# One written order for a whole fused attention and two-layer MLP program, in place of a written head and a scheduled rest

## The chip, the cores and the metric

The kernel runs on one core of a Trainium2 chip. The metric is device microseconds of one execution. The kernel before has a median of 858.6 us over three runs.

## The reference, cut to what matters

Nyström attention feeds two dense layers. Sizes: 4 batches, 8 heads, 576 positions, head size 64; 2304 tokens, width 512, inner width 2048.

```python
q_lm = q.reshape(B, H, 32, 18, D).mean(axis=3)
k_lm = k.reshape(B, H, 32, 18, D).mean(axis=3)
A, Bm, C = sm(q, k_lm), sm(q_lm, k_lm), sm(q_lm, k)   # row softmax, scale 1/8
Z = Bm.T / (norm1(Bm) * norminf(Bm) + 1e-6)
for _ in range(6):
    Z = 2 * Z - Z @ Bm @ Z
x = A @ Z @ C @ v            # heads side by side: [2304, 512]
h = x @ w_in;  g = h * tanh(softplus(h));  x = g @ w_out
h = x @ w2_in; g = relu(h) ** 2;           out = g @ w2_out
```

## The kernel before, in words

**Products.** The two MLP layers work on pairs of reduced-precision fp32 parts, a high and a low one ("h" and "l" in the tile names). Each product is three matmuls into one PSUM accumulation: high by high, low by high, high by low (`prod`, L685 to L687; the second layer's second product writes them out in L771 to L773).

**Attention.** Each batch has two groups of four heads; the eight groups are called a to h. A group's steps are: load q, k, v (`lq`, `lk`, `lv`), landmark sums on VectorE (`sq`, `sk`, L312 and L318), transposes on TensorE (`tq`, `tk`, `tl`) with ScalarE copies (`Tq`, `Tk`, `TL`), the three score products (`pa`, `pb`, `pc`), and the softmax pieces on VectorE, ScalarE and GpSimd (`at`, `am`, `mi`, `ae`, `su`, `mu`, `tb` for A; `cm`, `ce`, `cr`, `pe`, `ET`, `pv`, `cv` for C with v). `ah` and `al` split A into the two parts. A batch (B0 to B3) does the six Newton steps (`bx`, `be`, `bs`, `nr`, `rs`, then `n0` to `n5` on TensorE with `r` on ScalarE and `z` on VectorE) and `pw`, `wz`, which make the 64 x 64 factor of each head.

**Folds.** The product with w_in of the first layer is not made from x: each batch's small factors are multiplied into w_in, for each of four column groups of 512 (`Fold`, F00 to F33: batch, column group). `fo` is eight calls of a 64 x 32 by 64 x 512 matmul (L662, 16 instructions in the trace), on different parts of the array; `mh` (ScalarE, L670) and `ml` (VectorE, L673) split the result.

**Turns.** The MLP work is 48 turns, t0 to t23 for layer one, t24 to t47 for layer two. A turn is one column group (512 of 2048) and one block of 384 tokens. Its four `f` steps make h in PSUM (two banks, each for two f); `M` is the activation on ScalarE (L737), `c` and `g` split it (L746 or L749 on ScalarE, L755 on VectorE, with a square on VectorE, L747, in layer two). The `y` steps (four in layer one, three in layer two) multiply with w_out into a PSUM buffer of which there are two, shared with attention steps; `e` adds it to an accumulator in SBUF (L793, L795, L797). The last column group of layer one also splits x (L804 on ScalarE, L805 on GpSimd), that of layer two also stores (four DMAs, L811).

**Weights.** 64 weight units (U0 to U63: for each layer and column group four of w_in and four of w_out) come in a raw 64-bit form. `d` loads 512 KB on SP's queue; `lo` (ScalarE, L200), `st` (VectorE, L203), `ab` (ScalarE L210, or VectorE L212 when the unit is "beside"), `cl` (VectorE, L216 and L217) and `ad` (GpSimd, L223 or L227) turn them into fp32; `hi` (ScalarE, L232) and `lw` (GpSimd, L238) split them. The raw form has two buffers of its own; the split parts have 24.

**Who orders the work.** Every engine takes its instructions in order, and SP's queue issues the loads and stores in order. In the kernel before, the list `PROGRAM` (641 steps) gives the order by hand up to the last f of turn 7; each word is a thing, a step, behind "@" the PSUM buffer and behind "+" a number of extra matmuls that keep TensorE going. Then a loop over turns 8 to 47 emits folds (`folded`), fronts (f, M, c, g), backs (y, e) and, by the due times in `WHEN`, weight units from 16 on (`wturn`, whole units through `all`). What stands outside `tc.manual_schedule()` is put in order by the framework's scheduler, by a timeline that it works out itself; it may place these instructions between those of the list.

Of the kernel before, what the change touches and what calls it, by code (L numbers as in the profile page):

```python
# [46 lines left out]


PROGRAM = """
    a.lk U0.d@m a.lq a.sk a.tk@h a.Tk U1.d@m a.Sk U0.lo a.lv a.sq a.tq@h a.Tq b.lk U0.st a.Sq U1.lo a.tl@y U0.ab  # L50
    U2.d@m U1.st a.TL U0.cl U1.ab a.pb@y b.lq a.pa@at b.sk U0.ad a.PB a.pc@h U3.d@m U2.lo b.tk@h a.cm b.Sk a.at
    a.ce b.lv a.am b.Tk a.pe@at a.cr a.mi b.sq U4.d b.tq@h a.ET a.ae a.pv@y c.lk b.Tq a.su a.cv b.Sq U2.st U3.lo
    b.tl@y U5.d a.mu U2.ab b.TL c.lq a.tb U4.lo b.pc@h+4 U3.st a.ah b.pb@at U4.st U6.d@gh c.tk@h+3 U3.ab U2.cl
    U4.ab a.al b.cm b.PB U5.lo c.lv c.tq@at+2 c.sk b.ce U2.ad c.Tq b.pe@h d.lk U6.lo b.pa@at B0.bx U4.cl B0.be
    U7.d@gl b.ET B0.bs c.Sk b.pv@y+1 c.Tk b.at U4.ad d.lq B0.nr@y b.am U4.hi d.tk@h B0.rs U7.lo d.Tk U1.cl
    B0.n0@at+5 d.lv d.tq@h U4.lw B0.r0 B0.z0 c.sq B0.n1@y d.Tq b.mi U8.d B0.r1 U1.ad B0.z1 b.ae b.cr B0.n2@at+2
    d.sq e.lk b.cv B0.r2 c.Sq c.tl@y c.TL B0.z2 b.su B0.n3@y+2 U8.lo c.pb@at e.lq B0.r3 e.tk@h B0.z3 c.PB U7.st
    d.Sq U3.cl B0.n4@y U7.ab c.pc@h b.mu B0.r4 B0.z4 d.sk B0.n5@y c.pa@at U3.ad f.lk e.Tk B0.z5 e.lv d.Sk U7.cl
    B0.pw@y+3 d.tl@y B0.wz U7.ad b.tb F00.fo@h f.lq d.TL c.at U7.hi d.pb@y c.am b.ah d.pc@at U7.lw c.cm F00.mh
    d.cm b.al c.ce f.lv F00.ml d.ce f.tk@h+4 c.mi c.cr d.PB d.cr t0.f0 f.Tk B1.bx U5.st d.pe@at c.ae U6.st B1.be  # L60
    t0.f1 d.ET c.su U6.ab d.pv@y B1.bs x.m t0.M0 t0.f2 U6.cl B1.nr@y e.sq d.cv U6.ad t0.c0 d.pa@at c.mu c.pe@h
    U6.hi x.e U5.ab t0.f3 B1.rs d.at U6.lw B1.n0@y+2 e.Sq c.ET B1.z0 f.tq@at d.am B1.r0 x.m t0.M1 U5.cl B1.n1@y
    c.pv@y d.mi B1.z1 c.tb t0.c1 e.tq@h t0.g0 B1.r1 c.cv t0.g1 B1.n2@y x.e d.ae B1.z2 U5.ad e.sk B1.r2 U5.hi
    B1.n3@y+4 U5.lw B1.r3 B1.z3 d.su e.Sk f.Tq B1.n4@y+3 e.tl@y U9.d B1.r4 B1.z4 c.ah d.mu f.sk B1.n5@at t0.y0
    e.Tq c.al e.TL d.tb t0.y1 t0.e0 B1.z5 U9.lo U8.st f.Sk d.ah U9.st B1.pw@y U8.ab f.sq d.al e.pc@h t0.e1
    e.pb@at U9.ab t0.y2 e.PB B1.wz f.Sq U9.cl F10.fo@h e.cm t0.e2 U9.ad f.tl@at F10.mh U8.cl U10.d t0.y3 f.TL
    U8.ad F10.ml e.ce f.pa@at t0.e3 e.cr f.pc@h f.at U11.d U10.lo e.pe@h f.cm e.pa@at e.ET U10.st f.pb@y g.lk
    f.ce f.am e.pv@y f.PB f.mi U10.ab f.cr f.pe@h e.at U11.lo t1.f0 U10.cl f.ae f.ET B2.bx t1.f1 g.lq f.su
    U10.ad B2.be e.cv g.tk@at x.m t1.M0 B2.bs U12.d t1.f2 f.mu g.sk t1.c0 g.lv B2.nr@y f.pv@y g.Tk f.tb t1.f3
    f.cv t1.g0 g.Sk U12.lo t2.f0 t1.M1 U12.st t1.c1 g.tq@at U11.st x.e U11.ab t2.f1 t1.g1 e.am t1.y0 B2.rs x.m  # L70
    t2.M0 U11.cl B2.n0@y t2.f2 B2.z0 t2.c0 g.sq U11.ad t2.f3 t1.e0 e.mi U13.d B2.r0 g.Tq F01.fo@h t2.g0 x.e e.ae
    F11.fo@at t1.y1 F01.mh e.su F11.mh t1.y2 F01.ml e.mu t1.e1 x.m t2.M1 F11.ml B2.n1@y t3.f0 B2.z1 e.tb B2.r1
    t2.c1 B2.n2@at t3.f1 B2.z2 B2.r2 t2.g1 e.ah t3.f2 f.ah e.al B2.n3@y t1.e2 t3.f3 B2.z3 B2.r3 U13.lo f.al
    B2.n4@at t3.M1 t1.y3 B2.z4 B2.r4 x.e U12.ab U13.st t2.y0 U13.ab U12.cl t1.e3 U13.cl g.Sq t2.y1 t2.e0 U13.ad
    x.m t3.M0 U12.ad t4.f0 U13.hi B2.n5@at t2.e1 U13.lw t4.f1 U12.hi t3.c0 B2.z5 t4.f2 U14.d t3.c1 U12.lw t4.f3
    t3.g0 B2.pw@y t3.g1 t4.M0 t2.y2 B2.wz U15.d U14.lo t4.M1 U14.st F20.fo@at x.e U14.ab g.tl@y t5.f0 U15.lo
    U14.cl t5.f1 F20.mh U15.st t5.f2 U14.ad F20.ml U15.ab t5.f3 g.TL U15.cl U14.hi g.pa@at t2.e2 U15.ad t2.y3
    g.at h.lk U14.lw U15.hi g.am g.pb@y U15.lw t2.e3 g.pc@at t4.c0 g.cm g.mi h.lq t4.c1 t3.y0 h.sk g.ce g.ae
    h.tk@at g.PB t3.e0 h.Sk t3.y1 h.Tk h.lv h.sq h.tq@at t3.e1 h.Sq g.su h.tl@y h.Tq t3.y2 h.TL t4.g0 t4.g1 x.m
# [850 lines left out]
```

## Time and profile before

| What | Value |
|---|---|
| median of three runs | 858.6 us (857.69 to 862.78) |
| profiled execution, span | 856.0 us |
| granted TensorE clock, mean | 0.995 |
| TensorE busy | 818.3 us |
| VectorE busy | 455.4 us |
| ScalarE busy | 363.9 us |
| GpSimd busy | 198.1 us |

The span goes from the first to the last instruction of one execution. PE is TensorE's matmuls, PEld its weight loads, DVE VectorE, ACT ScalarE, POOL GpSimd, SP SyncE, which issues the DMAs. Matmuls are pipelined, so the duration of one is longer than the distance to the next; starts are compared, not durations.

### The profile page before, as it was taken

The page shows a single profiled execution, that of the slowest core. Times are in us where ns is not written, and L with a number is a line of the kernel's source. Part 1 is how long each engine was busy: PE and PEld are TensorE (multiplying, and loading weights), DVE is VectorE, ACT ScalarE, POOL GpSimd, SP SyncE. Part 2 cuts the span into 40 slices and gives each one's busy share as a digit, 9 for nine tenths or more (in the row PEclk, how much of TensorE's full clock was granted, in tenths as well). Part 3 has the DMA queues.
Part 4 walks back from the last instruction along what each step waited for, and adds up shares of the span by engine and source line. Part 5 has one row for each costly group of instructions (what it writes and reads, how often), then busy time and mean ns, then how long its engine had stood idle before and what let it go on. Part 6 is the DMA issues. An engine that isn't in the chain of part 4 may idle for free.

```text
span 856.0 us, 13523 instructions
## 1 busy us (share of the span) xinstructions
PE 818.3 (96%) x5646; PEld 732.6 (86%) x5646; DVE 455.4 (53%) x721; ACT 363.9 (43%) x578; POOL 198.1 (23%) x179
## 2 busy tenths in 40 slices
PE   4778999798999999999999999999999999999997
PEld 3657788687997989898999899899989989999996
DVE  5899865765346655247434633744345553534332
ACT  4668797643453434244734413533233421321120
POOL 1434323222032232016533301331023300300000
PEclk9999999999999999999999999999999999999999
DMA  9951503203033111011101100211011300101112
GB/s 245 312 164 27 158 27 129 53 3 99 1 99 99 50 50 50 1 50 50 50 1 50 50 1 28 72 49 50 1 50 50 99 0 1 50 1 50 50 50 74
DMA packets 25916, 53.29 MB, mean 62 GB/s; under 512 B 3072, under 2 KB 15360, under 8 KB 25856
## 3 DMA queue, kind: packets, MB, share of 16 engines
...
q14 instruction: 16, 0.13, 0.0%
...
## 4 chain that ended last, share of the span: by engine, by line
PE 75%; DMA 9%; DVE 6%; issue 4%; POOL 2%; ACT 2%; SPq 1%; ACTq 0%; POOLq 0%; DVEq 0%
PE h L685 11%; PE h L687 11%; PE h L686 11%; PE y L772 8%; PE y L773 8%; PE y L771 8%; PE y L685 6%; PE y L686 6%; PE y L687 6%; DMA rawwo<-in_moe_w_out_dram 4%; DMA rawwi<-in_moe_w_in_dram 3%; DMA q<-in_q_dram 2%; PE m L662 2%; DVE gl L755 1%; SPq L192 1%
## 5 line engine op out<-in xcount | busy, mean ns | idle before, releaser
L737 ACT ACTIVATE s<-h 128x768 f32<-128x768 f32 x96 | 77.5, 807 | 189.4 <-PE h L687 186.0
L755 DVE TENSOR_TENSOR gl<-s,gh 128x768 fp32r<-128x768 f32 x96 | 97.6, 1020 | 40.9 <-ACT gh L749 40.3
L747 DVE TENSOR_TENSOR s<-s 128x768 f32<-128x768 f32 x48 | 47.5, 991 | 86.4 <-ACT gh L746 86.0
L685 PE MATMUL h<-ah,mh 128*128 128x384 f32 (+1 forms) x256 | 80.0, 313 | 0.0
L687 PE MATMUL h<-ah,ml 128*128 128x384 f32 (+1 forms) x256 | 78.4, 306 | 0.4 <-DVE ml L673 0.4
L686 PE MATMUL h<-al,mh 128*128 128x384 f32 (+1 forms) x256 | 78.0, 305 | 0.0
L797 DVE TENSOR_TENSOR o<-o,y 128x512 f32<-128x512 f32 x54 | 37.0, 685 | 70.0 <-PE y L773 69.2
L797 DVE TENSOR_TENSOR acc<-acc,y 128x384 f32<-128x384 f32 x72 | 39.3, 549 | 54.4 <-PE y L687 54.1
L227 POOL TENSOR_TENSOR rawwo<-rawwo 128x512 int32<-128x512 int32 x32 | 36.8, 1151 | 101.0 <-DVE rawwo L217 76.7
L685 PEld LDWEIGHTS h<-ah,mh 128*128 128x128 f32 x256 | 48.5, 190 | 6.0 <-issue 2.5
L687 PEld LDWEIGHTS h<-ah,ml 128*128 128x128 f32 x256 | 48.6, 190 | 2.4 <-issue 1.7
L686 PEld LDWEIGHTS h<-al,mh 128*128 128x128 f32 x256 | 48.6, 190 | 0.8 <-issue 0.8
L749 ACT CAST gh<-s 128x768 fp32r<-128x768 f32 x48 | 39.6, 834 | 18.7 <-PE y L687 17.9
L203 DVE SCALAR_TENSOR_TENSOR rawwo<-rawwo 128x512 uint32<-128x512 uint32 x32 | 26.7, 838 | 34.4 <-ACT rawwo L200 31.7
L203 DVE SCALAR_TENSOR_TENSOR rawwi<-rawwi 128x512 uint32<-128x512 uint32 x32 | 22.0, 687 | 39.2 <-ACT rawwi L200 36.6
L746 ACT ACTIVATE gh<-s 128x768 fp32r<-128x768 f32 x48 | 40.5, 845 | 1.2
L200 ACT ACTIVATE rawwi<-rawwi 128x512 f32<-128x512 uint32 x32 | 21.6, 675 | 43.1 <-DMA rawwi<-in_moe_w_in_dram 41.9
L200 ACT ACTIVATE rawwo<-rawwo 128x512 f32<-128x512 uint32 x32 | 21.7, 677 | 41.8 <-DMA rawwo<-in_moe_w_out_dram 41.7
L805 POOL TENSOR_TENSOR xl<-acc,xh 128x384 fp32r<-128x384 f32 x24 | 26.3, 1100 | 33.6 <-ACT xh L804 33.6
L223 POOL TENSOR_TENSOR wi<-rawwi 128x512 int32<-128x512 int32 x16 | 16.7, 1046 | 70.6 <-DVE rawwi L217 59.4
L227 POOL TENSOR_TENSOR rawwi<-rawwi 128x512 int32<-128x512 int32 x16 | 19.9, 1247 | 52.8 <-DVE rawwi L217 48.3
L662 PE MATMUL m<-wi,wz 64*32 64x512 f32 x256 | 24.5, 601 | 0.1
...
## 6 DMA issues: line engine op xcount, KB each, us to landing
rawwo<-in_moe_w_out_dram SPq DMA_DIRECT2D x32, 512.0 KB, 3.9
...
rawwi<-in_moe_w_in_dram SPq DMA_DIRECT2D x16, 512.0 KB, 3.7
...
k<-in_k_dram SPq DMA_DIRECT2D x4, 576.0 KB, 4.3
q<-in_q_dram SPq DMA_DIRECT2D x4, 576.0 KB, 6.5
...
```

The costliest lines, as they stand in the source:

```text
L203: nc.vector.scalar_tensor_tensor(self.low, self.up, 0x80000000, self.low, ALU.bitwise_and, ALU.bitwise_or)
L227: nc.gpsimd.tensor_tensor(up, up, low, ALU.add)
L685: nc.tensor.matmul(ps, wh, rh, start=start, stop=False)
L686: nc.tensor.matmul(ps, wh, rl, start=False, stop=False)
L687: nc.tensor.matmul(ps, wl, rh, start=False, stop=stop)
L737: nc.scalar.activation(s, self.hs[hf][:, :, :TT], AF.Relu if self.li else AF.Mish)
L747: nc.vector.tensor_tensor(s, s, s, ALU.mult)
L755: nc.vector.tensor_tensor(self.gl[:, sl, :], self.s[hf], self.gh[:, sl, :].bitcast(F32), ALU.subtract)
L771: nc.tensor.matmul(ps, gh, W.oh[f][:, 0, :], start=(i == 0), stop=False)
L772: nc.tensor.matmul(ps, gh, W.ol[f][:, 0, :], start=False, stop=False)
L773: nc.tensor.matmul(ps, gl, W.oh[f][:, 0, :], start=False, stop=(i == FG - 1))
L797: nc.vector.tensor_tensor(a, a, ps, ALU.add)
```

## The change

The loop, `WHEN`, `TURN`, `folded`, `wturn`, `front` and `back` go. `PROGRAM` now names all 1834 steps of the program, and all of it stands inside `tc.manual_schedule()`. Steps that had done work on two engines are cut: `q` (the square on VectorE) comes out of `c`; `xh` and `xl` (the split of x) and `o` (the stores) come out of `e`. `x.two` swaps the SBUF pools between the layers. Units 16 to 39 are marked "beside" (`ab` on VectorE); before, the loop marked those that it emitted in layer one. The head of the list is in a new order too: among other things the loads begin a.lq, a.lk, b.lk, U0, b.lq, U1, U4, U2, U3, c.lk, where they began a.lk, U0, a.lq, U1, a.lv, b.lk, U2, b.lq, U3, b.lv. No instruction of the computation is added or removed.

```diff
-TURN = 8
-WHEN = [
...
 PROGRAM = """
-    a.lk U0.d@m a.lq a.sk a.tk@h a.Tk U1.d@m a.Sk U0.lo a.lv a.sq a.tq@h a.Tq b.lk U0.st a.Sq U1.lo a.tl@y U0.ab
...
-    t7.M1 t7.c1 t7.g1 t6.y3 t6.e2 t6.e3
+    a.lq a.lk a.sq b.lk a.tq@h a.Sq a.Tq a.sk a.Sk U0.d@m b.lq U1.d@m a.tk@h a.tl@y a.Tk a.TL U0.lo a.pa@at U4.d
...
+    U15.lo h.lv B2.r4 U15.st t4.f1 U15.ab B2.n5@at t3.c1 U12.lw x.m B2.z5 t2.e1
...
+    t2.y3 t2.e2 U14.cl U17.d g.pc@at g.am g.cm U14.ad U14.hi t2.e3 t4.c0 t5.f3 U14.lw t3.y0 x.e h.Sk g.ce g.mi
+    U17.lo h.tk@at t3.e0 g.ae t4.g0 f.ah h.Tk t5.M1 t3.y1 h.tq@at f.al h.tl@y t3.e1 g.su g.mu h.Tq t3.y2 h.TL t3.e2
...
+    t18.y3 U34.st U34.ab U34.cl U34.ad U34.hi U34.lw t20.f3 t18.xl2 F33.fo@at t19.g1 F33.mh t19.y0 t20.c0 t18.e3
...
+    t47.c0 t43.o1 t47.q0 t46.y0 t46.y1 t47.c1 t46.e0 t47.g0 t46.e1 t47.q1 t46.y2 t47.g1 t46.e2 t46.o0 t47.y0 t47.y1
+    t47.e0 t46.o2 t47.e1 t47.y2 t46.o1 t47.o0 t47.o1 t47.e2 t47.o2
 """
...
-    def folded(b, fg):
-        if (b, fg) not in folds:
-            x = Fold(b, fg)
-            x.fo()
-            x.mh()
-            x.ml()
...
             if self.li:
                 nc.scalar.activation(gh, s, AF.Square)
-                nc.vector.tensor_tensor(s, s, s, ALU.mult)
...
+        def q(self, hf):
+            s = self.s[hf]
+            nc.vector.tensor_tensor(s, s, s, ALU.mult)
...
+        def xh(self, k):
...
+        def xl(self, k):
...
+        def o(self, k):
...
+        def two(self):
+            nonlocal l2
+            l1.release()
+            l2 = ctx.enter_context(tc.tile_pool(name="l2", bufs=NT, reuse_waits="tile"))
...
+    for u in units[16:BESIDE]:
+        u.beside = True
...
-    def wturn(t):
-        n = 16
-        for a, e in WHEN:
-            n += 4 if t >= e else max(0, min(4, math.ceil(4 * (t - a) / (e - a))))
-        while done[0] < min(n, len(units)) and len(free["w"]) > (not units[done[0]].by_rows):
-            units[done[0]].beside = t < len(ORDER)
-            units[done[0]].all()
-            done[0] += 1
...
-    for i, w in enumerate(turns + [None]):
...
```

## Rows read from the trace of the kernel before

**Rows 1.** The page's part 1: busy time, share of the span, instructions.

```profile
PE 818.3 (96%) x5646; PEld 732.6 (86%) x5646; DVE 455.4 (53%) x721; ACT 363.9 (43%) x578; POOL 198.1 (23%) x179
```

**Rows 2.** By stage: length, busy us of PE, PEld, DVE, ACT, POOL; clock; DMA.

```profile
0.00:60.19 60.19, 39.20 (x534) 28.44 (x535) 47.72 (x89) 33.95 (x72) 19.78 (x28) 1.00 0.91 256
60.19:106.20 46.01, 41.71 (x637) 34.65 (x636) 41.91 (x84) 36.21 (x72) 16.76 (x16) 0.96 0.32 85
106.20:206.00 99.80, 92.44 (x916) 78.84 (x916) 64.57 (x126) 63.95 (x114) 27.17 (x26) 0.98 0.20 57
206.00:280.00 74.00, 73.52 (x466) 67.18 (x467) 35.78 (x59) 34.65 (x51) 16.44 (x14) 1.00 0.26 72
280.00:851.40 571.40, 571.40 (x3100) 523.52 (x3098) 264.69 (x366) 195.12 (x270) 117.96 (x95) 1.00 0.13 40
```

**Rows 3.** TensorE's timeline around a whole fold: start us, us, line, out<-in.

```profile
406.76 0.34 PE L687 MATMUL h<-ah,ml 128*128 128x384 f32 x1
407.02 1.09 PE L662 MATMUL m<-wi,wz 64*32 64x512 f32 x16
...
408.32 0.34 PE L685 MATMUL h<-ah,mh 128*128 128x384 f32 x1
```

**Rows 4.** TensorE's timeline: first cut fold, one cut fold, the last one.

```profile
257.82 1.05 PE L662 MATMUL m<-wi,wz 64*32 64x512 f32 x4
...
300.23 0.34 PE L687 MATMUL h<-ah,ml 128*128 128x384 f32 x1
300.50 1.05 PE L662 MATMUL m<-wi,wz 64*32 64x512 f32 x4
...
301.76 0.34 PE L686 MATMUL y<-gl,wo_8h 128*128 128x384 f32 x1
...
305.60 0.34 PE L687 MATMUL y<-gh,wo_11l 128*128 128x384 f32 x1
305.87 1.08 PE L662 MATMUL m<-wi,wz 64*32 64x512 f32 x12
...
307.15 0.34 PE L686 MATMUL h<-al,mh 128*128 128x384 f32 x1
...
392.97 1.07 PE L662 MATMUL m<-wi,wz 64*32 64x512 f32 x10
```

**Rows 5.** VectorE's first sums, the loads' sizes (page, part 6), the weight step L203.

```profile
5.14 2.12 DVE L318 TENSOR_REDUCE lmk<-k 128x64 f32<-128x1152 f32 x1 [3.33 <-DMA k<-in_k_dram]
9.87 2.13 DVE L318 TENSOR_REDUCE lmq<-q 128x64 f32<-128x1152 f32 x1 [2.61 <-DMA q<-in_q_dram]
...
rawwi<-in_moe_w_in_dram SPq DMA_DIRECT2D x16, 512.0 KB, 3.7
...
q<-in_q_dram SPq DMA_DIRECT2D x4, 576.0 KB, 6.5
...
L203 DVE SCALAR_TENSOR_TENSOR rawwo<-rawwo 128x512 uint32<-128x512 uint32 x32 | 26.7, 838 | 34.4 <-ACT rawwo L200 31.7
```

**Rows 6.** Timelines of ScalarE and TensorE, 155 to 206 us; in brackets the wait before.

```profile
155.24 0.67 ACT L200 ACTIVATE rawwi<-rawwi 128x512 f32<-128x512 uint32 x1 [2.38 <-DMA rawwi<-in_moe_w_in_dram]
156.67 1.44 PE L346 MATMUL tk<-ident,k 128*128 128x128 f32 x8 [2.64 <-ACT E L424]
158.23 0.52 PE L686 MATMUL y<-gl,wo_4h 128*128 128x384 f32 x1
160.47 0.45 PE L687 MATMUL y<-gh,wo_6l 128*128 128x384 f32 x1
167.78 0.45 PE L685 MATMUL y<-gh,wo_4h 128*128 128x384 f32 x1 [2.05 <-DVE acc L797]
199.92 0.69 ACT L200 ACTIVATE rawwi<-rawwi 128x512 f32<-128x512 uint32 x1 [4.78 <-DMA rawwi<-in_moe_w_in_dram]
206.00 0.45 PE L685 MATMUL y<-gh,wo_0h 128*128 128x384 f32 x1 [2.26 <-DVE acc L797]
```

**Rows 7.** VectorE's last instruction.

```profile
851.44 0.69 DVE L797 TENSOR_TENSOR o<-o,y 128x512 f32<-128x512 f32 x1 [2.03 <-PE y L773]
```

More of the change, by code (lines that the diff above doesn't have):

```diff
@@ L32 @@
 NW = 24
+BESIDE = 40
 IN_PAGES = ((1, 0), (1, 1), (2, 0), (2, 1))
@@ L781, in e @@
             li, fg, n = self.li, self.fg, self.n
-            last = fg == NFG - 1
             ps = self.ys[k]
@@ L798, in e @@
             give(f"y{self.nm}{k}")
-            if last and li == 0:
-                if k % 2 == 0:
-                    for t, x in zip("hl", xs.setdefault(n, ([], []))):
-                        x.append(page(f"x{t}{n}{k // 2}", F32R))
-                xh, xl = (t[k // 2][:, k % 2, :] for t in xs[n])
-                nc.scalar.copy(xh, a)
-                nc.gpsimd.tensor_tensor(xl, a, xh.bitcast(F32), ALU.subtract)
-                if k % 2:
-                    give(f"acc{n}{k // 2}")
-            elif last:
-                for m in range(P // LM):
-                    b, i = divmod((n * TT + k * P) // LM + m, SEG)
-                    nc.sync.dma_start(
-                        out[b * S : (b + 1) * S, :].rearrange("(l i) d -> i l d", i=SEG)[i],
-                        a[m * LM : (m + 1) * LM, :],
-                    )
-        def front(self):
-            for k in range(FG):
-                self.f(k)
-                yield
-                if k % 2:
-                    self.M(k // 2)
-                    self.c(k // 2)
-                    self.g(k // 2)
-        def back(self):
-            for k in range(TT // P if self.li else NCC):
-                self.y(k)
-                self.e(k)
-                yield
+        def xh(self, k):
+            n = self.n
+            if k % 2 == 0:
+                for t, x in zip("hl", xs.setdefault(n, ([], []))):
+                    x.append(page(f"x{t}{n}{k // 2}", F32R))
+            nc.scalar.copy(xs[n][0][k // 2][:, k % 2, :], acc[n, k // 2][:, k % 2, :])
+        def xl(self, k):
+            n = self.n
+            xh, xl = (t[k // 2][:, k % 2, :] for t in xs[n])
+            nc.gpsimd.tensor_tensor(xl, acc[n, k // 2][:, k % 2, :], xh.bitcast(F32), ALU.subtract)
+            if k % 2:
+                give(f"acc{n}{k // 2}")
+        def o(self, k):
+            n, a = self.n, outs[self.n][:, k, :]
+            for m in range(P // LM):
+                b, i = divmod((n * TT + k * P) // LM + m, SEG)
+                nc.sync.dma_start(
+                    out[b * S : (b + 1) * S, :].rearrange("(l i) d -> i l d", i=SEG)[i],
+                    a[m * LM : (m + 1) * LM, :],
+                )
     class Tables:
@@ L852, in nystrom_mish_relu2 @@
     things["x"] = Tables()
+    for u in units[16:BESIDE]:
+        u.beside = True
+    l2 = None
     with tc.manual_schedule():
```

170 lines of the change are left out of this document (106 added, 64 removed).

## The prediction, made before the result was known

> **What bounds the kernel now.** I read the page's shares first. TensorE is busy 96% of the span, VectorE 53%, ScalarE 43% [rows 1]. In a kernel like this the only time that can be won without removing work is TensorE's idle time and the matmul time that is badly used, so the second view was busy time by stage [rows 2]. From 280.00 us to 851.40 us TensorE is busy for all 571.40 us of it: no order of the list can remove idle time there. The idle time lies in front. Up to 60.19 us, where the first layer-1 product starts, it is 60.19 - 39.20 = 21.0 us; then 46.01 - 41.71 = 4.3 us; then 99.80 - 92.44 = 7.4 us up to 206 us; then 0.5 us. The rest of the 856.0 us span is the tail: the last product ends near 851.4 us, VectorE adds it in 0.69 us, and its four stores land at the end, 4.6 us in all [rows 7]. The tail keeps its form in the new list (last y, last e, last o), so it cancels.
>
> VectorE is the engine behind the first two stages: it is busy 47.72 of 60.19 us and 41.91 of 46.01 us [rows 2]. What it is handed first decides when TensorE gets its products. In the third stage it has room (64.57 of 99.80 us), and what matters there is who stands in front of whom in its queue.
>
> **Term 1, the folds.** The third view was TensorE's own timeline. A fold's matmuls go to different 64x32 parts of the array side by side, so a fold costs the time of one part. Where a fold stands whole (x16), from the h in front of it at 406.76 to the second h behind it at 408.32 there are 1.56 us [rows 3]. Take off two product intervals. One interval is 0.1745 us: from 301.76 to 305.60 there are 22 products [rows 4]. A whole fold therefore costs 1.56 - 0.35 = 1.21 us. In the part that the scheduler orders, a fold is cut in two by a pair of y groups: a piece of x4 and a piece of x12. The x4 piece costs 301.76 - 300.23 - 0.35 = 1.18 us, the x12 piece 307.15 - 305.60 - 0.35 = 1.20 us [rows 4]. A piece costs as much as the whole. There are seven such cut folds of the sixteen, the first with its x4 at 257.82, the last with its x10 at 392.97 [rows 4]. In the new list `fo` is one step, its eight calls stand together in the written order, and TensorE takes them so. Gain: 7 x (1.18 + 1.20 - 1.21) = 7 x 1.17 = 8.2 us. All seven lie behind 206 us, where TensorE is idle for 0.5 us in all [rows 2], so nothing hides this; it is on the path. Bounds: 7 x 1.0 and 7 x 1.2.
>
> **Term 2, the start.** The old list issues a.lk, then 512 KB of weights (U0), then a.lq. VectorE gets k at 5.14 us and q only at 9.87 us, after an idle wait of 2.61 us [rows 5]. These two transfers of 512 and 576 KB take 4.73 us, 230 KB/us. The new list issues a.lq, a.lk, b.lk and then U0. The second tensor then comes 576/230 = 2.5 us after the first: 2.2 us earlier. Against that, more VectorE work is listed ahead of t0.f0: U5.st and U6.st have moved in front of it, 2 x 0.838 us [rows 5], and B1.bx, while c.cr and d.cr have moved behind. Two y weights alone take back 1.7 of the 2.2 us for the first product. Ahead of t1.f0 both lists have the same weight steps, and the new one has e.at, e.cr and f.cr behind it, so there the 2.2 us stand. I take 2.0 us. Bounds: a loss of 1.7 us (the loads gain nothing, the two steps cost) and a gain of 4.3 us (all the idle time of the second stage [rows 2]). The v loads move behind e.lk; pv is needed only for B0.pw, at the end of the Newton chain, which hides them.
>
> **Term 3, the stalls between 106 and 206 us.** Three gaps make up 6.9 of the 7.4 us. At 156.67 tk waited 2.64 us for E of ScalarE, at 167.78 a y waited 2.05 us and at 206.00 another 2.26 us for VectorE's acc [rows 6]. In front of the first and the last, ScalarE sat 2.38 and 4.78 us in front of `lo` (L200) of a w_in unit until its load landed [rows 6]. The last w_in unit of the old list is U11, and U12 to U15 are w_out: so these are units from 16 on, from the loop behind the list, which the scheduler moved up into it. ScalarE and VectorE take their work in order, so E and acc stood behind them. After the first gap the clock fell: from 158.23 to 160.47 seven products take 0.32 us each, where they take 0.1745 else [rows 6, 4]. That is about the half level, 1.2 against 2.4 GHz, with a granted clock of 0.98 over the whole stage [rows 2]. Ten such products lost 1.4 us. Together 6.9 + 1.4 = 8.3 us.
>
> The new list names every one of these units. U17.lo stands behind g.ce, and between the step that frees its buffer (U15.lw) and U17.lo there are 8.7 us of listed TensorE work; the tk of group h is no longer behind an unlanded load. h.lk stands 12 us of TensorE work ahead of h.tk. So I expect the three old gaps gone. But a list that names all units has its own tight places. Of the 48 units from 16 on, I count 16 with under 5 us of listed TensorE work between the step that frees the raw buffer and the `lo` (U34, U36, U42, U51, U59 and U61 have none), while L200 waits for landings of some 4 us. Each holds ScalarE, and VectorE behind it, until the load is there. Whether TensorE notices depends on the next acc: a y group lasts 2.72 us (0.69 us of e and 2.03 us of wait for the next [rows 7]), and two buffers stand between a y and the e that frees it. The bound from below is nothing, as after 280 us in the old trace, where such waits exist and TensorE never stops. The bound from above is 16 x 2.2 = 35 us at the price of one old gap. I take two new gaps of 2.2 us, because in the old trace such units made three gaps, all in the stage in which VectorE also has attention to do, and the new list has two of them (U16, U17) ahead of t6.f3, where that stage ends. Net: 8.3 - 4.4 = 3.9 us.
>
> **Edits at nothing.** Splitting q from c, xh and xl from e, and o from e moves no work to another engine and adds no instruction; L747 ran behind L746 before and has 3 us or more of products as cover. The warm matmuls are 35 in both lists. The set of ScalarE table loads changes by a few of 1.3 us, on an engine that is 57% idle. The order of the o steps at the end (t46.o2 ahead of t46.o1) makes SP wait for one e; three y groups of 2.72 us still stand between that e and the last one, as cover. BESIDE = 40 gives `ab` of units 16 to 39 to VectorE, as the loop did for units taken during the first layer's turns.
>
> **Sum.** 856.0 - 8.2 - 2.0 - 3.9 = 841.9 us of span. The median of the runs, 858.6 us, is 2.6 us above the profiled span; I carry that over: 844.5 us, 1.6% faster. About 1% is what a measurement of this kernel can tell from no change.
>
> **The clock as an added price.** After the 2.64 us gap the rows show about half rate for some 3 us, after the 2.26 us gap at 206 us they show none: the stage that begins there has a granted clock of 1.00 [rows 2, 6]. The Trainium skill (TensorE: Matmul & The Clock Gate, section "HAM oscillation — how this bites in real kernels") says that idle time between bursts sends the clock back to its half level, so that the next burst starts slow; the trace agrees at 157 us and not at 206 us. By that rule each of my two new gaps would also cost 1.4 us, and the sum would be 847.3 us.
>
> **Rivals.**
> *Only the folds.* The new gaps equal the old ones and the start gains nothing: 856.0 - 8.2 + 2.6 = 850.4 us. For it: old and new list are nearly alike up to t7.f0 in what stands ahead of what. Against it: the three gaps have a cause that the new order takes away.
> *All of it.* No new gap, and the whole idle time of the second stage goes: 856.0 - 8.2 - 4.3 - 8.3 + 2.6 = 837.8 us. For it: 571 us without a gap in the old trace although weights wait for loads there too.
> *Slower: weights hold the queues.* The 16 tight units each stop TensorE for 2.2 us, since a written order lets no later step pass a waiting `lo` or `st`. 856.0 - 8.2 - 2.0 - 8.3 + 35.2 + 2.6 = 875.3 us. It turns slower than before once 9 of the 16 do so (18.5 / 2.2 = 8.4). For it: L200's waits of 2.38 and 4.78 us in front of real gaps. Against it: y buffers and the room of VectorE after 206 us (it is busy 264.69 of 571.40 us [rows 2]).
> *The folds stay cut.* If the written order did not bind TensorE, term 1 would vanish: 852.7 us. Against it: the folds named in the old list are all x16.
>
> **Chances.** Forecast 0.50, only the folds 0.21, all of it 0.17, weights hold 0.10, folds stay cut 0.02. The forecast spreads over 839 to 850 us. Range 833 to 858 us: below, the "all of it" case and 5 us of the first stage's idle time; above, the folds alone with some new gaps. Faster by over 1% (under 850.0): nearly all of the forecast, "all of it" and a fifth of "only the folds", 0.70. Within 1%: 0.21. Slower by over 1%: 0.09.
>
> **What would show it.** Folds: sixteen pieces of x16, none of x4 to x12. Start: q and k on VectorE about 2.5 us apart, the first h at 58 to 60 us. Stalls: no TensorE wait of 2 us between 106 and 206 us with an L200 in front; idle time after 280 us not over 5 us. I am wrong if TensorE waits for acc or s in many places after 206 us, with L200 waiting for a load ahead of each, or if a fold's time in one piece is near 2.4 us.

## The result, and the profile after

The kernel after takes 825.13 us (median of four runs, 824.35 to 827.35); the kernel before took 858.14 us beside it (856.20 to 862.78). The ratio is 0.961, 95% interval 0.957 to 0.966. The prediction was 844.5 us with a range of 833 to 858: the sign was right, the gain of 33 us is more than twice the 14 us forecast, and it lies outside the range. The profiled span is 822.8 us, against 856.0.

The page's part 1 of the kernel after, to be read beside [rows 1]:

```profile
PE 802.0 (97%) x5646; PEld 730.1 (89%) x5646; DVE 447.1 (54%) x721; ACT 368.3 (45%) x588; POOL 201.7 (25%) x179
```

The same instructions on TensorE, and yet 16 us less busy time. The rest of the gain is idle time, and the view by stages tells where (columns as in [rows 2]; the stages are cut at the first layer-1 product and at like places behind it):

```profile
0.00:53.99 53.99, 38.38 (x535) 28.52 (x535) 47.11 (x86) 35.56 (x75) 18.33 (x27) 0.94 1.01 269
53.99:94.00 40.01, 39.41 (x576) 33.84 (x575) 35.10 (x79) 32.58 (x65) 17.52 (x16) 1.00 0.42 114
94.00:190.00 96.00, 96.00 (x1034) 84.87 (x1033) 65.48 (x131) 67.49 (x116) 30.38 (x28) 1.00 0.22 67
190.00:260.00 70.00, 70.00 (x464) 65.80 (x462) 33.85 (x52) 37.09 (x55) 12.59 (x10) 1.00 0.18 52
260.00:818.20 558.20, 558.18 (x3048) 517.03 (x3046) 264.82 (x375) 195.55 (x279) 122.88 (x98) 1.00 0.14 43
```

Length less TensorE's busy time, stage by stage, before and after: 21.0 and 15.6 us, 4.3 and 0.6, 7.4 and 0, 0.5 and 0. The first product begins at 53.99 us, 6.2 us earlier and ahead of the 58 to 60 us that the prediction gave as a sign. From 94 us to the end of its last product TensorE is idle for 0.02 us in all, though ScalarE goes on waiting for weight loads, 28.7 + 30.7 = 59 us over the two kinds of weights (before, 41.9 + 41.7 = 84 us). The groups of instructions of ScalarE's first weight step (before it was L200, now L267):

```profile
L267 ACT ACTIVATE rawwi<-rawwi 128x512 f32<-128x512 uint32 x32 | 21.6, 676 | 28.7 <-DMA rawwi<-in_moe_w_in_dram 28.7
L267 ACT ACTIVATE rawwo<-rawwo 128x512 f32<-128x512 uint32 x32 | 21.4, 671 | 30.7 <-DMA rawwo<-in_moe_w_out_dram 30.7
```

The folds (L662 before, L729 now) are all whole: x16, or two together as x32. TensorE's timeline of the kernel after around one pair and one single fold, beside [rows 3, 4]:

```profile
171.48 1.95 PE L729 MATMUL m<-wi,wz 64*32 64x512 f32 x32
...
363.04 0.34 PE L746 MATMUL h<-ah,ml 128*128 128x384 f32 x1
363.31 1.09 PE L729 MATMUL m<-wi,wz 64*32 64x512 f32 x16
364.33 0.44 PE L744 MATMUL y<-gh,wo_12h 128*128 128x384 f32 x1
```

VectorE's first sums, which stood at 5.14 and 9.87 us with waits in front [rows 5], now follow one another without a wait behind the first load:

```profile
4.42 2.13 DVE L385 TENSOR_REDUCE lmq<-q 128x64 f32<-128x1152 f32 x1 [2.59 <-DMA q<-in_q_dram]
6.46 4.17 DVE L385 TENSOR_REDUCE lmk<-k 128x64 f32<-128x1152 f32 x2
```

The tail is what it was [rows 7], 822.8 - 818.2 = 4.6 us:

```profile
818.22 0.69 DVE L858 TENSOR_TENSOR o<-o,y 128x512 f32<-128x512 f32 x1 [2.03 <-PE y L835]
```

One can go further and add up, from TensorE's timeline, the distance from each start to the next, idle time taken off, by kind of product. Before and after: idle time 33.1 and 16.1 us, folds 22.8 and 15.7, the 128x384 products 480.4 and 473.5, attention 63.9 and 61.8. The four differences are 17.0 + 7.1 + 6.9 + 2.1 = 33.1 us, the gain of the span. The other kinds move by 0.2 us at most.

### The profile page after: what moved, and what is told of

The parts are those of the page before. It is cut to its first block, busy times and chain, and to the rows that moved or that the text cites. A ratio compares the mean times of both kernels' runs of the same rounds, so it can differ in the third digit from the quotient of the medians.

```text
span 822.8 us, 13540 instructions
## 1 busy us (share of the span) xinstructions
PE 802.0 (97%) x5646; PEld 730.1 (89%) x5646; DVE 447.1 (54%) x721; ACT 368.3 (45%) x588; POOL 201.7 (25%) x179
## 4 chain that ended last, share of the span: by engine, by line
PE 91%; DMA 5%; DVE 2%; SPq 0%; ACT 0%; issue 0%; DVEq 0%
PE h L744 13%; PE h L746 12%; PE h L745 12%; PE y L744 8%; PE y L834 8%; PE y L835 8%; PE y L833 8%; PE y L746 8%; PE y L745 8%; DMA rawwo<-in_moe_w_out_dram 3%; PE m L729 2%; DMA rawwi<-in_moe_w_in_dram 1%; DMA q<-in_q_dram 1%; DMA v<-in_v_dram 1%; PE pv L517 0%; DVE q L379 0%
## 5 line engine op out<-in xcount | busy, mean ns | idle before, releaser
L817 DVE TENSOR_TENSOR gl<-s,gh 128x768 fp32r<-128x768 f32 x96 | 101.3, 1060 | 35.4 <-ACT gh L807 34.7
L811 DVE TENSOR_TENSOR s<-s 128x768 f32<-128x768 f32 x48 | 50.4, 1055 | 37.3 <-ACT gh L805 37.2
L267 ACT ACTIVATE rawwo<-rawwo 128x512 f32<-128x512 uint32 x32 | 21.4, 671 | 30.7 <-DMA rawwo<-in_moe_w_out_dram 30.7
L267 ACT ACTIVATE rawwi<-rawwi 128x512 f32<-128x512 uint32 x32 | 21.6, 676 | 28.7 <-DMA rawwi<-in_moe_w_in_dram 28.7
L270 DVE SCALAR_TENSOR_TENSOR rawwo<-rawwo 128x512 uint32<-128x512 uint32 x32 | 23.6, 740 | 15.7 <-ACT rawwo L267 12.3
L871 POOL TENSOR_TENSOR xl<-acc,xh 128x384 fp32r<-128x384 f32 x24 | 26.4, 1112 | 15.7 <-ACT xh L866 15.6
L270 DVE SCALAR_TENSOR_TENSOR rawwi<-rawwi 128x512 uint32<-128x512 uint32 x32 | 22.8, 713 | 13.7 <-ACT rawwi L267 9.6
L856 DVE COPY o<-y 128x512 f32<-128x512 f32 x18 | 12.2, 687 | 30.5 <-PE y L835 30.5
## 6 DMA issues: line engine op xcount, KB each, us to landing
v<-in_v_dram SPq DMA_DIRECT2D x16, 288.0 KB, 10.3
```

Of the source, the lines that this page charges most:

```text
L270: nc.vector.scalar_tensor_tensor(self.low, self.up, 0x80000000, self.low, ALU.bitwise_and, ALU.bitwise_or)
L811: nc.vector.tensor_tensor(s, s, s, ALU.mult)
L817: nc.vector.tensor_tensor(self.gl[:, sl, :], self.s[hf], self.gh[:, sl, :].bitcast(F32), ALU.subtract)
```

## The experiments

**e2: the new head with the scheduled rest.** The kernel before, with its listed steps in the new order (633 for 641: eight steps that only switch ScalarE's tables are left out).

```diff
-    a.lk U0.d@m a.lq a.sk a.tk@h a.Tk U1.d@m a.Sk U0.lo a.lv a.sq a.tq@h a.Tq b.lk U0.st a.Sq U1.lo a.tl@y U0.ab
...
+    a.lq a.lk a.sq b.lk a.tq@h a.Sq a.Tq a.sk a.Sk U0.d@m b.lq U1.d@m a.tk@h a.tl@y a.Tk a.TL U0.lo a.pa@at U4.d
...
```

> The new order for the 641 steps of the head, the rest left to the loop and the scheduler as before. Theory A: only the head's 10.3 us are won, 858.1 - 10.3 = 848 us, folds still cut into pieces of x4 and x12, and units from 16 on again in front of attention work with gaps of 2 us. Theory B: 858.1 - 25 = 833 us. Theory C: 858 us.

Measured: 842.22 us, ratio 0.981 (0.978 to 0.983). That lies between theories A and B. The head's order alone brings 858.1 - 842.2 = 15.9 us; the rest of the change brings the other 17.1. By stages, cut as above:

```profile
0.00:54.15 54.15, 38.64 (x534) 28.58 (x534) 46.65 (x86) 35.21 (x75) 18.28 (x27) 0.94 1.01 270
54.15:92.00 37.85, 37.25 (x562) 31.71 (x563) 33.78 (x75) 30.82 (x64) 17.47 (x16) 1.00 0.42 111
92.00:192.00 100.00, 95.56 (x1013) 83.28 (x1012) 69.28 (x138) 67.91 (x114) 28.95 (x28) 0.98 0.21 61
```

The first two stages are those of the kernel after; the third has 4.4 us of idle time again. Its largest gap shows how a unit that the scheduler has moved up does its harm. TensorE, ScalarE and VectorE of e2, from their timelines:

```profile
144.75 1.48 PE L344 MATMUL tk<-ident,k 128*128 128x128 f32 x7 [2.86 <-ACT E L422]
...
138.23 0.68 ACT L198 ACTIVATE rawwi<-rawwi 128x512 f32<-128x512 uint32 x1 [2.99 <-DMA rawwi<-in_moe_w_in_dram]
143.86 0.74 ACT L422 ACTIVATE E<-pc,mx 128x576 f32<-128x576 f32 x1 [3.03 <-DVE mx L417]
...
138.95 0.69 DVE L201 SCALAR_TENSOR_TENSOR rawwi<-rawwi 128x512 uint32<-128x512 uint32 x1 [1.95 <-ACT rawwi L198]
139.67 1.48 DVE L210 TENSOR_SCALAR rawwi<-rawwi 128x512 uint32<-128x512 uint32 x1
142.83 0.75 DVE L416 TENSOR_REDUCE mx<-pc 128x1 f32<-128x576 f32 x1
```

ScalarE waits 2.99 us for the load, VectorE waits with it, and then the unit's steps run on VectorE in one piece, from 138.95 to 142.83 us, in front of the maximum that E needs. Here it is the unit's steps on VectorE that stand in the way, and not its `lo` alone (e10, below, has the same `lo` at the same place without them). Folds are cut as before, seven of them.

**e3: the kernel after with seven folds cut.** `fo` of F12, F22, F32, F03, F13, F23 and F33 becomes two steps, with two y steps between them.

```diff
-        def fo(self, tag="at"):
...
-            for h in range(4):
+        def fp(self, tag):
+            self.ps = big(f"m{self.b}{self.fg}", tag)
+            self.part((0,))
+        def fq(self):
+            self.part((1, 2, 3))
+            self.used()
```

> The changed kernel with seven folds (F12, F22, F32, F03, F13, F23, F33) cut as before: two of the eight calls, then two product steps, then the other six. If a piece costs as much as a whole fold (theory A): 825.1 + 7 x 1.18 = 833.4 us. Rival: a cut costs only the change from one kind of weights to the other, some 0.3 us a time: 827 us.

Measured: 835.43 us, ratio 0.973 (0.970 to 0.976), 10.3 us over the kernel after. The first cut fold on its TensorE timeline:

```profile
236.56 1.05 PE L741 MATMUL m<-wi,wz 64*32 64x512 f32 x4
...
240.88 1.08 PE L741 MATMUL m<-wi,wz 64*32 64x512 f32 x12
```

In its profile the first product begins at 55.62 us, 1.6 us later than in the kernel after, in a stretch that the edit doesn't touch (in e8, which has the order of the kernel after, it begins at 54.44). The two spans differ by 833.0 - 822.8 = 10.2 us, so 8.6 us fall to the cuts, where term 1 had 8.2. By kinds of product the folds take 22.5 us, as before the change, against 15.7, and the 128x384 products 475.1 against 473.5; these 8.4 us are nearly all of it.

**e4: the kernel before with `fo` inside `tc.manual_schedule()`.**

```diff
-            x.fo()
+            with tc.manual_schedule():
+                x.fo()
```

> The kernel before with one edit: the fold's eight calls of the loop are kept together, the scheduler orders all else. Theory A: 858.1 - 8.2 = 850 us, sixteen folds of x16 and the three gaps of 2 us between 106 and 206 us still there. Rival (the cut is not what costs, or the scheduler pays for the whole fold elsewhere): 856 to 860 us.

Measured: 859.63 us, ratio 1.002 (0.999 to 1.005). The folds stayed cut (x4 and x12, x6 and x10), so the edit tells nothing of what whole folds are worth.

**e1 and e7: the old head with the written rest.** In e1 the old list stands first and all that is not in it follows in the new order. In e7 the steps of the rest that the new list has among the head's (units 16 to 21, F21, the first of t8) stand among them again.

```diff
 PROGRAM = """
-    a.lq a.lk a.sq b.lk a.tq@h a.Sq a.Tq a.sk a.Sk U0.d@m b.lq U1.d@m a.tk@h a.tl@y a.Tk a.TL U0.lo a.pa@at U4.d
+    a.lk U0.d@m a.lq a.sk a.tk@h a.Tk U1.d@m a.Sk U0.lo a.lv a.sq a.tq@h a.Tq b.lk U0.st a.Sq U1.lo a.tl@y U0.ab
...
```

> The head of the list (641 steps, to the last f of turn 7) in the old order, the rest named in the new order, folds whole, nothing placed by the scheduler. Theory A (the gain of 33 us comes from three places: the folds 8.2, the order of the head 10.3, being the 6.2 us by which the first h comes earlier and some 4.1 us of idle time up to 112 us, and the rest from units that no longer stand in front of attention work): 825.1 + 10.3 = 835.4 us, first h near 60 us, no gap of 2 us between 106 and 206 us. Theory B (all but the folds is the head's order): 858.1 - 8.2 = 850 us. Theory C (the head's order is worth nothing): 825 us.

> The kernel after with the head's 641 steps in the order of the list before, as in e1, but the named steps of the rest that the new list puts among the head's (units 16 to 21, F21, the first steps of t8) stand among them at the matching places and not behind the whole head. Theory A: e1's loss was its seam, and the folds and the written rest bring 15 to 17 us whatever the head's order: 841 to 845 us, no gap over 2 us behind 106 us, first h at 60 to 62 us. Rival: named units among the old head's steps stop TensorE as the moved-up ones did: 848 us or more, with gaps of 2 us or more between 106 and 230 us.

Measured: e1 860.39 us, ratio 1.002 (1.000 to 1.004), above all three of its theories; e7 846.18 us, ratio 0.984 (0.980 to 0.988), between its theory and the rival. In e1 the whole gain of the rest is lost in one place. TensorE, ScalarE and VectorE of e1:

```profile
233.62 1.96 PE L729 MATMUL m<-wi,wz 64*32 64x512 f32 x16 [17.18 <-DVE ml L740]
...
231.05 0.65 ACT L267 ACTIVATE rawwi<-rawwi 128x512 f32<-128x512 uint32 x1 [5.29 <-DMA rawwi<-in_moe_w_in_dram]
...
231.74 0.69 DVE L270 SCALAR_TENSOR_TENSOR rawwi<-rawwi 128x512 uint32<-128x512 uint32 x1 [8.45 <-ACT rawwi L267]
```

VectorE stands behind one weight unit after another, each behind its load, and the fold's `ml` behind VectorE: 17.18 us without a product. This is the rival "weights hold the queues", made by hand at the seam of two lists. In e7 the seam is gone and so are 14 us; three gaps of 1.0 to 1.9 us are left between 150 and 220 us. The first and the last stand behind a `lo` (of the last, ScalarE's row first, then TensorE's):

```profile
215.04 0.65 ACT L267 ACTIVATE rawwi<-rawwi 128x512 f32<-128x512 uint32 x1 [4.88 <-DMA rawwi<-in_moe_w_in_dram]
...
216.44 0.44 PE L744 MATMUL h<-ah,mh 128*128 128x384 f32 x1 [1.86 <-ACT s L796]
```

VectorE has no work between 210.7 and 216 us there: the `lo` alone holds the activation behind it, and with it TensorE. So a written order has such places or has none, as it is written. The first product of e7 comes at 60.66 us, as before the change.

**e5 and e6: only the loads.** e5 is the kernel after with the first 20 loads in the old order, e6 the kernel before with the new order of the first ten; from the eleventh on, where the new list has c.lq, e6 goes on with a.lv, b.lv and the rest in the old order (in both, the tensor that VectorE sums first stays first).

```diff
 e5, order of the loads
-a.lq a.lk b.lk U0 b.lq U1 U4 U2 U3 c.lk c.lq d.lq d.lk b.lv U7 e.lk a.lv ...
+a.lq U0 a.lk U1 a.lv b.lk U2 b.lq U3 b.lv U4 c.lk U5 c.lq U6 c.lv d.lk ...
 e6, order of the loads
-a.lk U0 a.lq U1 a.lv b.lk U2 b.lq U3 b.lv U4 c.lk U5 c.lq U6 c.lv d.lk ...
+a.lk a.lq b.lk U0 b.lq U1 U4 U2 U3 c.lk a.lv b.lv U5 c.lq U6 c.lv d.lk ...
```

> The kernel after, with the first 20 loads on SP's queue in the order of the list before (a.lq still first: a.lq U0 a.lk U1 a.lv b.lk U2 b.lq U3 b.lv U4 c.lk ...), each issued no later than the step that reads it; no other step is moved. Theory A: the 16 us of the head come from the order of the loads, since VectorE's idle time in front of the first h is time in which it waits for data. Then most of them go: 836 to 842 us, first h at 59 to 62 us, and VectorE waits of 2 to 3 us for k and q are back. Rival B: the order of the steps on VectorE, ScalarE and TensorE makes it, and the loads are early enough in either order: 825 to 830 us, first h at 54 to 56 us.

> The kernel before, with the first 20 loads in the order of the new list (a.lk a.lq b.lk U0 b.lq U1 U4 U2 U3 c.lk c.lq d.lq d.lk b.lv ..., a.lk first as its a.sk is); no other step is moved. Theory A (the order of the loads): 842 to 848 us, first h at 54 to 56 us. Rival B (the order of the other steps): 854 to 859 us, first h at 58 to 60 us. Something between says that the two must go together.

The text of e6 above says the first 20 loads; in the kernel that ran only the first ten have the new order, and e9 and e12, which start from it, have the same loads.

Measured: e5 836.31 us, ratio 0.973 (0.969 to 0.977), 11.2 us over the kernel after, first product at 62.45 us. e6 858.53 us, ratio 1.001 (0.998 to 1.003), first product at 62.15 us. Neither theory holds for both: with the new steps the order of the loads is worth 11 us; with the old steps that of the first ten is worth nothing, and all 20 were not run. ScalarE's timeline of e6 shows why, and TensorE's first score product behind it:

```profile
10.14 0.65 ACT L199 ACTIVATE rawwi<-rawwi 128x512 f32<-128x512 uint32 x1 [2.36 <-DMA rawwi<-in_moe_w_in_dram]
10.70 0.99 ACT L355 COPY qT<-tq 128x1024 f32<-128x1024 f32 x1
14.02 0.65 ACT L199 ACTIVATE rawwi<-rawwi 128x512 f32<-128x512 uint32 x1 [2.19 <-DMA rawwi<-in_moe_w_in_dram]
15.13 0.37 ACT L376 COPY kT<-tl 128x256 f32<-128x256 f32 x1
...
15.82 0.28 PE L394 MATMUL pb<-kT,qT 64*32 64x32 f32 x4 [3.46 <-ACT qT L376]
```

q and k are there and their sums end at 8.7 us, but U0.lo and U1.lo stand in front of the copies on ScalarE, and their loads now come later. In the first 20 us VectorE is busy 15.43 us in the kernel after, 10.43 in e6, 10.45 before the change and 8.53 in e5.

**e9 and e12: e6 with single steps moved by hand.** e9 puts the first weight steps behind attention steps, about as the new list has them; e12 moves a's product with v behind the Newton steps as well.

```diff
 e9
-    a.lk a.lq b.lk a.sk a.tk@h a.Tk U0.d@m a.Sk U0.lo b.lq a.sq a.tq@h a.Tq U1.d@m U0.st a.Sq U1.lo a.tl@y U0.ab
+    a.lk a.lq b.lk a.sk a.tk@h a.Tk U0.d@m a.Sk b.lq a.sq a.tq@h a.Tq U1.d@m a.Sq a.tl@y U4.d a.TL U0.lo a.pb@y
...
 e12
-    a.ET a.ae a.pv@y b.lv b.Tq a.su a.cv b.Sq
+    a.ET a.ae b.lv b.Tq a.su b.Sq
...
-    B0.r4 B0.z4 d.sk
+    B0.r4 a.pv@y B0.z4 a.cv d.sk
```

> The kernel of e6 (before, with the new order of its first 20 loads) with the steps of the first weight units moved behind attention steps, about as in the new list: U0.lo behind a.TL, U0.st behind b.sk, U0.ab behind a.cm, U1.lo behind a.ce, U1.st, U1.ab, U0.cl and U0.ad behind a.mi, U2.lo behind a.cr. Theory A: in e6 the data came early and ScalarE let it lie, since U0.lo and U1.lo waited 2.4 and 2.2 us for their loads with the copies of a's q and k behind them. Then the score products begin 4 to 5 us earlier, and the first h and the end follow by 4 to 10 us: 848 to 854 us. Rival: the head is held further on by other steps, and the early gain is gone by the first h: 856 to 859 us.

> The kernel of e9 with one more pair moved: a.pv (TensorE) stands behind B0.r4 and a.cv behind B0.z4, near the end of B0's Newton steps as in the new list, and no longer in front of b's transposes, where in e9 TensorE stood 7.4 us for a's v, the seventeenth load of the new order. Theory A: this stand was the whole of what e9 lost; with it gone the first h comes at 54 to 58 us and the time is 846 to 853 us. Rival: old steps further down the list hold the head again (the gap goes, others grow): first h at 59 us or later, 854 to 859 us.

Measured: e9 858.55 us, ratio 1.001 (0.998 to 1.003), first product at 61.23 us; e12 857.76 us, ratio 0.999 (0.996 to 1.002), first product at 63.21 us: in both the rival holds. TensorE's timeline of e9, then of e12:

```profile
10.62 0.23 PE L394 MATMUL pb<-kT,qT 64*32 64x32 f32 x4 [0.74 <-ACT qT L376]
...
23.22 0.43 PE L449 MATMUL pv<-v,ET 96*32 96x64 f32 x4 [7.40 <-DMA v<-in_v_dram]
```

```profile
23.25 0.47 PE L369 MATMUL tl<-ident,lmq 128*128 128x128 f32 x1 [6.87 <-ACT lmq L331]
```

The first scores come 5 us earlier in e9 (10.62 us for 15.82), and the time is given back at once: TensorE stands 7.40 us for a's v, the eleventh load here (the text of e12 calls it the seventeenth, which it is in the new list). In e12 that wait is gone and TensorE stops at nearly the same moment, 23.25 us, for a copy of b's sums. That copy stood on ScalarE behind U2.lo, which waited for its load, and behind four more steps:

```profile
19.70 0.65 ACT L199 ACTIVATE rawwi<-rawwi 128x512 f32<-128x512 uint32 x1 [2.73 <-DMA rawwi<-in_moe_w_in_dram]
...
22.95 0.24 ACT L331 COPY lmq<-lmq 128x64 f32<-128x64 f32 x1
```

**e13 and e14: the head split by kind of step.** e13 takes the loads of a and b, units 0 to 6 and the products of a and b with v from the new list and the rest of the head from the old one; e14 the new attention steps with units 0 to 4, the loads of a to f and the products of a and b with v at their old places. "At its place" means behind the same number of attention steps of its engine.

```diff
 e13
-    a.lk U0.d@m a.lq a.sk a.tk@h a.Tk U1.d@m a.Sk U0.lo a.lv a.sq a.tq@h a.Tq b.lk U0.st a.Sq U1.lo
+    a.lk a.lq a.sk b.lk a.tk@h a.Tk a.Sk a.sq a.tq@h U0.d@m b.lq U1.d@m a.Tq a.Sq a.tl@y a.TL U0.lo
...
 e14
-    a.lk U0.d@m a.lq a.sk a.tk@h a.Tk U1.d@m a.Sk U0.lo a.lv a.sq a.tq@h a.Tq b.lk U0.st a.Sq U1.lo
+    a.lq U0.d@m a.lk a.sq a.tq@h a.Sq U1.d@m a.Tq U0.lo a.lv a.sk U0.st a.Sk a.tk@h b.lk a.tl@y a.Tk U1.lo
...
```

> The kernel before; the attention and Newton steps of the head keep the old order, and on every engine all steps of units 0 to 6, the first loads of q, k and v, and the two products with v of groups a and b stand where the new list has them (behind the same number of attention steps of that engine); a.lk stays ahead of a.lq. Theory A (both orders must go together): 853 to 859 us, first h at 58 us or later. Theory B (the supply carries it: no lo, st or cl stands ahead of attention work whose data are there): 843 to 849 us, first h at 54 to 56 us.

> The kernel before; the attention and Newton steps of the head in the new order, and on every engine the steps of units 0 to 4 and the loads of groups a to f where the old list has them (behind the same number of attention steps of that engine); a.lq stays ahead of a.lk. Theory A (both orders must go together): 851 to 859 us, first h at 58 us or later. Rival to it (the attention order carries it by itself): 843 to 849 us, first h at 54 to 56 us.

Measured: e13 863.64 us, ratio 1.005 (1.003 to 1.008), first product at 60.08 us; e14 867.02 us, ratio 1.010 (1.006 to 1.013), first product at 68.80 us. Both lie above the ranges of their theories. Neither mixture of old and new gains anything, they cost half a per cent and one per cent; the whole new order of the head brings 16 us (e2). One TensorE row of each (e13, then e14):

```profile
32.66 0.77 PE L572 MATMUL nrm<-inv,bones 128*128 128x128 f32 x2 [3.04 <-DVE inv L564]
```

```profile
49.06 0.65 PE L604 MATMUL nw__501<-inv 32*32 32x64 f32 x16 [4.70 <-DVE inv L594]
```

In both the first Newton steps wait for VectorE, which is at work on sums and weight steps of later use in front of them.

**e10: two `lo` moved up in the kernel after.**

```diff
-    ... U14.cl U17.d g.pc@at ... g.mi U17.lo h.tk@at ... U16.d t4.y1 ... g.ah U16.lo B3.pw@at
+    ... U14.cl U17.d U17.lo g.pc@at ... g.mi h.tk@at ... U16.d U16.lo t4.y1 ... g.ah B3.pw@at
```

> The kernel after with two steps of ScalarE moved up, as the scheduler had done in the kernel before: U17.lo stands right behind U17.d (17 steps earlier, in front of g.ce) and U16.lo right behind U16.d (in front of B3.r4). The order on the other engines stays. Theory A: a lo whose load is on its way holds what stands behind it on ScalarE: waits of 1 to 4 us of ScalarE for these loads, a TensorE gap of 1 to 3 us behind at least one of them, 826.5 to 831 us. Rival: TensorE has products enough listed there: no gap over 0.6 us, 825 to 826.3 us.

Measured: 826.84 us, ratio 0.963 (0.960 to 0.965). Of the two, U16.lo still finds its load there; U17.lo waits for it, and TensorE doesn't stop (ScalarE's timeline):

```profile
139.44 0.68 ACT L267 ACTIVATE rawwi<-rawwi 128x512 f32<-128x512 uint32 x1 [3.09 <-DMA rawwi<-in_moe_w_in_dram]
```

Behind 54 us there is no gap over 0.6 us: the rival holds in what it says of TensorE, with a time 0.5 us above its range. At this place a late `lo` by itself, with the unit's VectorE steps left where they were, is covered: E follows at 141.90 us, 1.6 us behind the maximum, and the tk behind it begins at 142.91 without a wait. Of the 1.7 us over the kernel after, 1.2 lie ahead of the first product, which comes at 55.17 us and not at 53.99, where the edit changes nothing.

**e8: U17.d moved down to U17.lo.**

```diff
-    ... U14.cl U17.d g.pc@at ... g.ce g.mi U17.lo
+    ... U14.cl g.pc@at ... g.ce g.mi U17.d U17.lo
```

> The kernel after with one step moved: U17.d stands right in front of U17.lo (behind g.mi, in front of h.tk) and not 17 steps earlier. Theory A: a lo that waits for its load among attention steps is what made the gaps of before, since E and the copies of the next group stand behind it on ScalarE: ScalarE sits 2 to 4 us in front of that lo, and TensorE stops for 1 to 4 us soon after, with some products at half rate: 826.5 to 831 us. Rival: the products listed there cover it as they cover such waits later on: no TensorE gap over 0.5 us, 825 us within 0.7.

Measured: 825.96 us, ratio 0.961 (0.958 to 0.963). The edit was void: no other load stands between the two places, each engine takes only its own steps from the list, and so the order on every engine stayed what it was. It is a second measurement of the kernel after, 0.8 us from the first.

**e11: an attempt at less.** TensorE still waits 2.2 us for E at 13 us; `a.cm` goes in front of `a.at` and U0.st behind it.

```diff
-    b.sk U0.st a.pc@h U2.d@m a.at x.m a.cm
+    b.sk a.pc@h a.cm U2.d@m a.at U0.st x.m
```

> The kernel after with a.cm moved in front of a.at and U0.st behind it on VectorE, so that E of group a can come some 1.5 us earlier and with it the product that TensorE waits 2.2 us for at 13 us. Theory A: the stretch up to the first h is bound by VectorE's work as a whole, which has no idle time there after 4.4 us but for fractions: the gap at 13 us shrinks and others grow, 824.5 to 826.3 us. Rival: that wait is on the path: 822.5 to 824 us.

Measured: 826.67 us, ratio 0.963 (0.960 to 0.965): no gain, and above both ranges. VectorE waits for the product in front of the maximum, and E comes later, not earlier (15.72 us for 14.30): U0.ab on ScalarE stands in front of E and waits for U0.st, which the edit itself moved back. The first product comes at 54.81 us. VectorE, then ScalarE:

```profile
12.85 0.76 DVE L485 TENSOR_REDUCE mx<-pc 128x1 f32<-128x576 f32 x1 [1.94 <-PE pc L477]
...
15.15 0.66 ACT L277 ACTIVATE rawwi<-rawwi 128x512 f32<-128x512 f32 x1 [1.16 <-DVE rawwi L270]
15.72 0.72 ACT L491 ACTIVATE E<-pc,mx 128x576 f32<-128x576 f32 x1
```

So the run doesn't tell whether an earlier E would gain time. In the kernel after, too, ScalarE is the last in front of E: the maximum is done at 13.21 us, and two table loads (at 10.92 and 12.43 us, 1.28 us each) and U0.ab stand ahead of E until 14.30. Moving those was not tried.

No version here is better than the kernel after.

## Why the prediction was wrong, step by step

**Term 1, the folds (8.2 us), was right.** All sixteen are whole, and cutting seven of them again costs 8.6 us net of the start (e3), 6.8 of them on the folds and 1.6 on the products beside them.

**Term 2, the start (2.0 us, bounds -1.7 to 4.3), failed, and with it the forecast.** The step that failed is the one that went from "the second tensor comes 2.2 us earlier" to the gain of the whole head. The second sum did begin earlier, by 9.87 - 6.46 = 3.4 us. (The v loads do not all move behind e.lk: b.lv stays ahead of it.) The step followed two loads and the weight steps on VectorE up to the first products, and took for the upper bound the second stage's idle time alone. Measured, the head's order is worth 15.9 us (e2). In the traces of before and e2 the idle time falls by 21.0 - 15.5 = 5.5 us in the first stage, 4.3 - 0.6 = 3.7 in the second and 7.4 - 4.4 = 3.0 in the third; the other 3.7 us or so are products and attention steps that take less time. The granted clock doesn't tell the two heads apart: from before to e2 it goes from 1.00 to 0.94 in the first stage and from 0.96 to 1.00 in the second [rows 2], but in e4, which has the old head, it is 0.94 and 1.00 as well. The 21.0 us of the first stage stood in [rows 2], and they should have been in the bound: what fills them is decided by what stands in front of what on five queues, and one load's arrival says little of it. e6 shows this best: q and k did come early, as term 2 had it (the second sum begins at 6.57 us), and the gain was nothing.

What the order of the head does is now known in parts and not by a single step. Its loads are needed (e5 loses 11.2 us without them); the first ten of them are worth nothing alone (e6), nor with the weight steps and a's product with v moved by hand (e9, e12); loads and weight steps without the attention steps lose half a per cent, the attention steps without them one per cent (e13, e14). In e6, e9 and e12 the trace shows the head of a queue that waits for data not yet there, with other work behind it; in e13 and e14 it shows VectorE at work on what is needed later. Which of the steps matter most stays open, since each mixture has its own new waits.

**Term 3, the three gaps (8.3 us), was right in what goes and wrong in what comes.** All three are gone. The two new gaps of 2.2 us that I took off did not come: behind 54 us TensorE has no wait over 0.6 us, with all sixteen tight units in the list. The units named for the two gaps, U16 and U17, were not among the sixteen: U17 has the 8.7 us of listed work that the prediction itself counts, and U16 more. So 4.4 us of the miss are here.

The three old gaps were not of one kind. The first is the kind that term 3 described. The maximum was done at 152.8 us, and E stood on ScalarE right behind the `lo` of 155.24 us [rows 6]. In front of the last, VectorE worked off weight steps while the sum that TensorE waited for stood behind them; the second, at 167.78 us, also waited for a sum, behind activation and weight steps. VectorE's and ScalarE's rows of the kernel before, first gap, then VectorE's in front of the last:

```profile
151.87 0.76 DVE L418 TENSOR_REDUCE mx<-pc 128x1 f32<-128x576 f32 x1 [1.54 <-PE pc L410]
155.79 0.73 ACT L424 ACTIVATE E<-pc,mx 128x576 f32<-128x576 f32 x1
...
203.55 0.42 DVE L217 TENSOR_SCALAR rawwi<-rawwi 128x512 uint32<-128x512 uint32 x1
203.88 0.42 DVE L212 TENSOR_SCALAR rawwi<-rawwi 128x512 uint32<-128x512 uint32 x1
204.34 1.15 DVE L216 TENSOR_SCALAR rawwi<-rawwi 128x512 f32<-128x512 f32 x1
205.41 0.54 DVE L797 TENSOR_TENSOR acc<-acc,y 128x384 f32<-128x384 f32 x1
```

Two pairs of runs bear on the two kinds. With the old head, e7 has a `lo` that waits 1.46 us in front of the same E, and tk waits 1.72 us; e1 has no `lo` there, and tk does not wait. With the new head, e2 and e10 have a `lo` that waits 3 us at the same place: with the unit's VectorE steps in front of the maximum tk waits 2.86 us (e2), without them not at all (e10). So a late `lo` is neither harmless nor always harmful, and naming the units does not by itself remove the gaps: it depends on what stands behind the waiting step and how many products TensorE still has.

**The sum.** 8.2 + 2.0 + 3.9 = 14.1 us of span were forecast. Put the measured terms in their place and it reads 8.6 for the folds, 15.9 for the head (with 3 us of the third stage's gaps in it), and 8.5 us left for the rest of the gaps (4.4 us of idle time that e2 still has in its third stage) and for products that follow one another more closely: 33 us. This is one of two ways to divide it: with the written rest the new head brings 846.2 - 825.1 = 21.1 us (from e7 to the kernel after), and with the old head the written rest brings only some 12. The two orders gain together. The tail and the edits at nothing held: the tail is 4.6 us as before, and ScalarE's 588 instructions for 578 show nowhere in the time.

**The rivals.** "Only the folds" is excluded by e2. "All of it", 837.8 us, was nearest and still 12.7 us off: it too held the first stage's idle time fixed, which fell by 5.4 us, and most of the remainder is products and attention steps that take less time. "Weights hold the queues" is real, e1 pays 17.18 us for it in one place; in the new list it doesn't occur, and in e7 it does on a small scale. "The folds stay cut" is excluded by the rows.

**The clock.** The price that I set beside the sum for half rate behind two new gaps found no gap to act on: in the kernel after the granted clock is 1.00 in every stage from the first product on. It rested on the row at 157 us alone: the section of the Trainium skill cited there works with waits longer than my two gaps of 2.2 us. That the clock falls at a long gap is seen in e12: from 20 to 26.5 us it is at the half level, 0.50; TensorE had stopped at 16.4 us for 6.87 us. But it also falls where no gap is long: in the kernel after it is 0.50 from 35.8 to 39.1 us, and the longest gap of TensorE between 20 and 40 us is 1.14 us. The view by windows, e12, then two stretches of the kernel after:

```profile
20.00:26.50 6.50, 3.25 (x33) 2.48 (x33) 3.20 (x7) 6.24 (x13) 1.47 (x2) 0.50 1.08 276
```

```profile
20.00:40.00 20.00, 15.99 (x234) 12.61 (x238) 18.48 (x43) 12.25 (x29) 6.75 (x7) 0.91 1.06 296
35.80:39.10 3.30, 3.30 (x37) 2.94 (x28) 2.93 (x4) 0.43 (x2) 1.55 (x2) 0.50 1.07 246
```

The Trainium skill (TensorE: Matmul & The Clock Gate, section "HAM oscillation — how this bites in real kernels") says that the clock goes back to its half level when the engine waits long between bursts; the row of e12 agrees. What made it fall in the kernel after is not shown by any run here.
